# Fused layer norm, local attention and SwGLU on one core: QKV weight slices loaded in row halves, row 0's mean from two sums, and row 1's copies on ScalarE

## The chip, the cores and the metric

One core of one Trainium2 chip runs the whole program. The metric is the device time of one execution in microseconds (us). Before the change it is 503.36 us, the median of three runs (503.14 to 503.40).

## The reference

```python
xn = (x - mean(x)) / sqrt(var(x) + 1e-5)              # x: 2048 tokens x 576, bf16
q, k, v = xn @ wqkv                                   # wqkv: 576 x 1728; 32 heads of 18
logits[s, w] = q[s] . k[s - 2 w] * 18 ** -0.5         # w = 0..7, masked where s < 2 w
o[s] = sum_w softmax(logits)[s, w] * v[s - 2 w]
out = x + o @ wo + (silu(xn @ w_gate) * (xn @ w_up)) @ w_down     # hidden size 4608
```

Matmul inputs are bf16, sums are f32. The attention and the feed-forward part both start from the same normalised rows `xn`, and both results are added to `x`.

## The kernel before

The 2048 tokens are laid out as 16 "rows": partition p holds the tokens 16p to 16p+15, and row r is the tile of 128 tokens that are each partition's r-th. So a load of "x row r" is 128 partitions of 576 values (144 KB). The work has two stages. In the first, every row is normalised, transposed, and multiplied with the QKV weights. In the second, four groups of four rows (`NTT = 4`) go through gate and up matmuls (`g_pair`, line 582, matmul at line 600) in chunks of four blocks of 128 hidden units, and then through the down and output projections (`d_half`, line 615, matmul at line 629). Local attention runs on VectorE beside the matmuls (`chain`, line 400). The order of instructions on each engine is written out by hand; each engine takes its own in program order, and waits by semaphores.

The change concerns the first microseconds. What happens there, in the order of the code:

**Loads (lines 154 to 165).** DMAs are issued by two engines, each with its own queue: ScalarE ("ACT queue") and SyncE ("SP queue"). The QKV weight (576 rows by 1728 columns) is loaded in slices of 128 rows: slices 0 to 3 are one load of 432 KB each (line 149), slice 4 is the remaining 64 rows, brought in two loads, the first 864 columns to partitions 0 to 63 and the rest to partitions 64 to 127 (line 152, 108 KB each). The ACT queue gets x row 0 and then slice 1. The SP queue gets x row 1, slice 0, slice 2, x row 2, slice 3, the two pieces of slice 4, x row 3, and then three chunks of four x rows each (line 165, 576 KB each). The DMAs share eight semaphores in turn, so that an issue waits until the DMA eight places before it has landed.

**Warm-up.** TensorE multiplies constants (`warm_pe`, lines 171 to 177) until the first row is ready. ScalarE loads its table for the square root (line 166).

**Row 0 (lines 478 to 499).** Row 0 takes a short cut: it is only centred (mean subtracted) before the transpose, and the factor 1/std is applied later, when its QKV results are copied out of PSUM (`p_evac`, lines 365 and 367). VectorE takes the statistics of two halves of 288 columns and joins them (`ln_stats`: lines 214 and 218), subtracts the mean from the first 128 columns and then from the rest (`ln_center`, line 251); GpSimd centres the last 64 columns once more, as padding to 640 (line 256). TensorE transposes five blocks of 128 columns (`transp_pe`, line 262), ScalarE copies the results to SBUF in three copies (`copy_pt`, line 268) as the left operands of the QKV matmuls. Row 0 is also normalised in full (`ln_apply`, lines 240 and 243) into a buffer of its own, which a DMA transpose on the SP queue turns for the feed-forward stage (line 291).

**Row 1.** It gets its statistics, root (line 229), reciprocal (line 234) and normalising, is transposed on TensorE in three groups (column blocks 0 and 1, 2, 3 and 4), and the results are copied out by ScalarE, VectorE and ScalarE.

**QKV matmuls (line 301).** The result of a row is four PSUM tiles of 432 columns (`t` for row 0, `u` for row 1). TensorE's order is: row 0 with slice 0 (four matmuls), slice 1 (four), slice 2 for two tiles; row 1's first three transposes; row 0 with slice 2 for the other two tiles; row 1's last two transposes; row 1 with slice 0 (four); row 0 with slice 3 (four) and slice 4 (`p_row0_rest`, line 309); then the rest of row 1 (`p_row`, line 321), with row 2's transposes in its middle (`transp_halves`, line 274). PSUM has eight banks for all of this, so that row 1's tiles take the banks of the warm-up tile and of the two transpose tiles `pa` and `pb` once these are copied out.

**Rows 2 and on.** Row 2's statistics, root and normalising (lines 514 to 516) come just before the evacuation of row 0 in VectorE's order. From row 4 on the pattern is regular (lines 552 to 576).

**Later.** The V chunk of the last four rows is stored to DRAM in three pieces during the first gate and up chunk (line 672), with loads of `wd`, `wo` and the next `gu` around it.

In the profile the loads of x appear under the tile `wd` and the QKV weights under `hT`, since the buffers are shared; row 0's transposed operand is `PP`, its normalised copy `A`.

Of the kernel before, what the change touches and what calls it, by code (L numbers as in the profile page):

```python
# [10 lines left out]
f32 = mybir.dt.float32  # L11
ACT = mybir.ActivationFunctionType
ALU = mybir.AluOpType
# [4 lines left out]
P = 128  # L18
H, DH, W, DIL = 32, 18, 8, 2
D = H * DH  # L20
HALF = D // 2
# [4 lines left out]
DPAD = KT * P  # L26
# [44 lines left out]
def kernel(  # L71
# [11 lines left out]
    nc = tc.nc  # L83
# [6 lines left out]
    x_v = A_x.rearrange("b (p r) d -> p (b r) d", r=R)  # L90
    out_v = out.rearrange("b (p r) d -> p (b r) d", r=R)

    const = ctx.enter_context(tc.tile_pool(name="const", bufs=1))
# [19 lines left out]
    PP = big.tile([P, 2, RT * D], bf16, name="PP")  # L113
# [8 lines left out]
    wdf = wd[:].rearrange("p f j -> p (f j)")  # L122
    XC, XN = RT * D, RT * DPAD
    xc_b = [wdf[:, i * XC:(i + 1) * XC].rearrange("p (r d) -> p r d", d=D) for i in range(4)]
# [4 lines left out]
    wqkv = hTf[:, 0:12 * D].rearrange("p (k j) -> p k j", j=3 * D)  # L129
# [14 lines left out]
    def load_x(eng, j):  # L144
        eng.dma_start(xc_b[0][:, j:j + 1, :], x_v[:, j:j + 1, :])  # L145

    def load_w(eng, kt):
        if kt < 4:
            eng.dma_start(wqkv[:, kt, :], A_wqkv[kt * P:(kt + 1) * P, :])
        else:  # L150
            for i in range(2):
                eng.dma_start(wqkvr[64 * i:64 * i + 64, :], A_wqkv[4 * P:D, 2 * G * i:2 * G * (i + 1)])

    load_x(nc.scalar, 0)
    load_x(nc.sync, 1)
    load_w(nc.scalar, 1)
    load_w(nc.sync, 0)
    make_identity(nc, ident[:])
    load_w(nc.sync, 2)
    load_x(nc.sync, 2)  # L160
    load_w(nc.sync, 3)
    load_w(nc.sync, 4)
    load_x(nc.sync, 3)
    for c in range(1, 4):
        nc.sync.dma_start(xc_b[c], x_v[:, 4 * c:4 * c + 4, :])
    nc.scalar.activation(warm[:], eps_t[:], ACT.Sqrt)

    wp = ps.tile([P, 512], f32, name="warm_ps", tag="ps")
# [27 lines left out]
    def new_ps(name):  # L196
        return ps.tile([P, 512], f32, name=name, tag="ps")


    ln = {}  # L200

    def ln_open(c):
        mv = lns.tile([P, 4, 2], f32, name="mv")
        rstd = lns.tile([P, 4], f32, name="rstd")
        ln[c] = (xc_b[c], xn_b[c % 2], mv, rstd)

    sums = {}

    def ln_half(r, k):
        c, j = divmod(r, 4)  # L210
        xc, xn, mv, rstd = ln[c]
        if k == 0:
            sums[r] = lns.tile([P, 2, 6], f32, name="stats")
        nc.vector.bn_stats(sums[r][:, k, :], xc[:, j, k * HALF:(k + 1) * HALF])  # L214

    def ln_aggr(r):
        c, j = divmod(r, 4)
        nc.vector.bn_aggr(ln[c][2][:, j, :], sums[r][:].rearrange("p c s -> p (c s)"))

    def ln_stats(r, n=1):  # L220
        for i in range(r, r + n):
            ln_half(i, 0)
            ln_half(i, 1)
            ln_aggr(i)

    def ln_sqrt(r, n=1):
        c, j = divmod(r, 4)
        xc, xn, mv, rstd = ln[c]
        nc.scalar.activation(rstd[:, j:j + n], mv[:, j:j + n, 1], ACT.Sqrt, bias=eps_t[:], scale=1.0)

    def ln_recip(r, n=1):
        c, j = divmod(r, 4)
        rstd = ln[c][3]
        nc.vector.reciprocal(rstd[:, j:j + n], rstd[:, j:j + n])

    def ln_apply(r):
        c, j = divmod(r, 4)
        xc, xn, mv, rstd = ln[c]
        dst = xn[:, j] if r else xn0
        nc.vector.tensor_scalar(dst[:, 0:D], xc[:, j], mv[:, j, 0:1], rstd[:, j:j + 1],  # L240
                                op0=ALU.subtract, op1=ALU.mult)
        if r < 2:
            nc.gpsimd.tensor_scalar(dst[:, D:DPAD], xc[:, j, 512:D], mv[:, j, 0:1], rstd[:, j:j + 1],
                                    op0=ALU.subtract, op1=ALU.mult)
        else:
            nc.vector.tensor_copy(dst[:, D:DPAD], dst[:, 512:D])

    def ln_center(r, lo=0, hi=D):
        c, j = divmod(r, 4)
        xc, xn, mv, rstd = ln[c]  # L250
        nc.vector.tensor_scalar(xn[:, j, lo:hi], xc[:, j, lo:hi], mv[:, j, 0:1], None, op0=ALU.subtract)

    def ln_center_pad(r):
        c, j = divmod(r, 4)
        xc, xn, mv, rstd = ln[c]
        nc.gpsimd.tensor_scalar(xn[:, j, D:DPAD], xc[:, j, 512:D], mv[:, j, 0:1], None, op0=ALU.subtract)

    def transp_pe(r, kts, pt):
        c, j = divmod(r, 4)
        xn = ln[c][1]  # L260
        for i, kt in enumerate(kts):
            nc.tensor.transpose(pt[:, i * P:(i + 1) * P], xn[:, j, kt * P:(kt + 1) * P], ident[:])  # L262

    def xT_of(r):
        return xcT if r == 0 else xnT[:, :, r * P:(r + 1) * P]

    def copy_pt(eng, r, kts, pt):
        eng(xT_of(r)[:, kts[0]:kts[-1] + 1, :],
            pt[:, 0:len(kts) * P].rearrange("p (k t) -> p k t", t=P))

    def new_pt():
        return ps.tile([P, 8 * P], bf16, name="pt", tag="ps")
# [31 lines left out]
    def p_whole(r, t, kt, gs=range(NG)):  # L304
        for g in gs:
            p_mm(t, g, kt, None, r, kt == 0, False)

    def p_row0_rest(t):
        for i in range(2):
            for half in range(2):  # L310
                p_mm(t, i + 2 * half, 4, half, 0, False, True)
# [68 lines left out]
    def store(m, c, parts=1):  # L380
        st = stage[(2 * c + m - 1) % 4].rearrange("p r d -> p (r d)")
        n = XC // parts
        for i in range(0, XC, n):
            nc.sync.dma_start(kv_d[m - 1, c - 1, :, i:i + n], st[:, i:i + n])
# [82 lines left out]
    def normalize(r, n=1):  # L467
        ln_recip(r, n)
        for i in range(r, r + n):
            ln_apply(i)  # L470
            if i > 4:
                transp_dma(i)
# [3 lines left out]

    warm_pe(10, 1)
    ln_open(0)
    ln_stats(0)
    ln_center_pad(0)  # L480
    ln_center(0, 0, P)
    ln_sqrt(0)
    pa, pb = new_pt(), new_pt()
    transp_pe(0, (0,), pa)
    ln_center(0, P, D)
# [3 lines left out]
    ln_stats(1)  # L489
    ln_sqrt(1)  # L490
    copy_pt(nc.scalar.copy, 0, (3, 4), pb[:, 2 * P:])
    ln_recip(0)
    ln_apply(0)
    ln_recip(1)
    ln_apply(1)

    t = [new_ps("qkv_ps") for g in range(NG)]
    p_whole(0, t, 0)
# [2 lines left out]
    transp_pe(1, (0, 1), pt1)  # L501
    transp_pe(1, (2,), pa)
    copy_pt(nc.scalar.copy, 1, (0, 1), pt1)
    copy_pt(nc.vector.tensor_copy, 1, (2,), pa)
    p_whole(0, t, 2, (2, 3))
    transp_pe(1, (3, 4), pb)
    copy_pt(nc.scalar.copy, 1, (3, 4), pb)
    u = [None] * NG
    for g in (0, 2, 1, 3):
        u[g] = new_ps("qkv_ps")  # L510
        p_whole(1, u, 0, (g,))
    p_whole(0, t, 3)
    p_row0_rest(t)
    ln_stats(2)
    ln_sqrt(2)
    normalize(2)
    p_evac(0, t, (5, 0, 3, 2, 4, 1), dve=(5, 2))
    ln_half(3, 0)
# [88 lines left out]
    def g_evac(ch, j):  # L607
        t = ring_ps[j]
        sg = tmp.tile([P, TT], bf16, name="sg", tag="sg", bufs=3)
        uc = tmp.tile([P, TT], bf16, name="uc", tag="uc", bufs=3)  # L610
        nc.scalar.activation(sg[:], t[0][:], ACT.Silu)  # L611
        nc.scalar.copy(uc[:], t[1][:])  # L612
        nc.vector.tensor_tensor(hT[:, ch * FC + j, :], sg[:], uc[:], op=ALU.mult)  # L613
# [32 lines left out]
    for tt in range(NTT):  # L646
        for ch in range(NCH):
            it = tt * NCH + ch
            for p in range(2):
                g_pair(tt, ch, p)  # L650
                for j in (2 * p, 2 * p + 1):
                    g_evac(ch, j)
                    if it % NCH < NCH - 1 or p == 0:
                        dve.pump(1.4)
            if ch == NCH - 1:
                dve.drain(lambda: chains[0] > tt)
                for r in range(RT * tt, RT * tt + RT):
                    nc.sync.dma_start_transpose(oT[:, :, r * P:(r + 1) * P], QOP[:, r, :])
                for i in (0, 2):
                    nc.sync.dma_start(xr[:, i:i + 2, :], x_v[:, RT * tt + i:RT * tt + i + 2, :])  # L660
            if it + NSLOT < NTT * NCH:
                load_gu(it + NSLOT)
            if tt == 0:
                if 1 <= ch <= 7:
                    load_wd(ch - 1)
                if ch in (3, 4):
                    load_wd(11 - ch)
                for _ in range(3 if ch in (1, 2) else 2):
                    if wo_order:
                        load_wo(wo_order.pop(0))  # L670
                if ch == 0:
                    store(2, 3, 3)
            if ch == 1 and tt < NTT - 1:
                chain(tt + 1)
        for sub in range(0, RT, 2):
            t, fence = {}, {}
            for swap in range(2):
                for i in (sub, sub + 1):
                    d_half(tt, i, swap, t, fence)
                    if swap:  # L680
                        dve.pump(12.5 if i == sub else 4.0)
                        d_out(RT * tt + i, i, t[i])
# [30 lines left out]
```

## Time and profile before

| what | value |
|---|---|
| median of three runs | 503.36 us (503.14 to 503.40) |
| the profiled execution | 503.32 us |
| its span (first to last instruction) | 501.5 us |
| TensorE matmuls (PE) busy | 496.8 us, 99% |
| VectorE (DVE) busy | 329.0 us, 66% |
| ScalarE (ACT) busy | 200.6 us, 40% |
| granted TensorE clock | 1.0 |
| first QKV matmul | 6.01 us after the span's start |
| matmuls of line 301 (QKV) / 600 (gate, up) / 629 (down, out) | 50.1 / 280.4 / 146.4 + 22.9 us busy |

The page comes from one profiled execution. Its times are counted from the start of the span, which is 1.8 us shorter than the execution's time. A row of a time line reads: start, duration (of several merged instructions, their busy time together), engine, source line, operation, output tile, input tiles, shape, count, and in brackets how long the engine had been idle and what ended that. "SPq" and "ACTq" are instructions that issue DMAs; their duration is that of the issue, not of the transfer. In the table of stretches each line gives a stretch, the busy time of each engine with the number of instructions, and then the granted clock, the busy share of the 16 DMA engines and the GB/s that they moved. In the list of DMA issues the last number is the time from issue to landing.

### The profile page before, as it was taken

What the parts mean: (1) busy time and instruction counts of PE and PEld (TensorE: products, weight loads), DVE (VectorE), ACT (ScalarE), POOL (GpSimd) and SP (SyncE); (2) the same over time, 40 slices, a digit from 0 to 9 for tenths busy, and PEclk for the clock granted to TensorE, in tenths of its full rate; (3) what the DMA queues carried; (4) which work ended last, traced back from release to release, by engine and by line L of the source; (5) the groups of instructions that cost most, each with busy time, mean ns of one, the idle gap of its engine ahead of it and who ended that gap; (6) DMA issues with size and microseconds to landing.
All of it is one profiled execution on the core that took longest, in us unless ns stands there. A gap on an engine that the chain in (4) does not pass through costs nothing.

```text
span 501.5 us, 13267 instructions
## 1 busy us (share of the span) xinstructions
PE 496.8 (99%) x5795; PEld 282.8 (56%) x5795; DVE 329.0 (66%) x478; ACT 200.6 (40%) x415; POOL 2.6 (1%) x9
## 2 busy tenths in 40 slices
PE   8999999999999999999999999999999999999997
PEld 4555544444677644444777544445777444446775
DVE  5889597998999698999897139995980222221001
ACT  4756657645300255544300445557000454553000
POOL 2000000000000000000000000000000000000000
PEclk9999999999999999999999999999999999999999
DMA  8689989898731045535631154453700335442200
GB/s 322 164 207 228 320 268 294 260 318 272 186 114 61 25 147 185 190 112 174 166 106 47 30 182 154 131 189 110 181 26 14 106 110 177 159 126 39 76 14 25
DMA packets 77186, 75.42 MB, mean 150 GB/s; under 512 B 22708, under 2 KB 72528, under 8 KB 77128
## 3 DMA queue, kind: packets, MB, share of 16 engines
q1 hardware_dynamic: 76840, 73.98, 49.2%
q8 instruction: 45, 0.74, 0.7%
q10 hardware_dynamic: 288, 0.59, 0.3%
q14 instruction: 13, 0.11, 0.1%
HBM read 58.76 MB, written 5.90 MB: 129 GB/s over the span
## 4 chain that ended last, share of the span: by engine, by line
PE 98%; DMA 1%; DVE 0%; SPq 0%; issue 0%
PE g_ps L600 56%; PE d_ps L629 32%; PE qkv_ps L301 11%; DMA hT<-in_A_wqkv_dram 1%; DVE ot L643 0%; PE pt L283 0%; SPq L145 0%; PE pt L262 0%; PE warm_ps L262 0%
## 5 line engine op out<-in xcount | busy, mean ns | idle before, releaser
L600 PE MATMUL g_ps<-xnT,gu 64*128 64x512 bf16 x2592 | 280.4, 376 | 0.0
L600 PEld LDWEIGHTS <-gu 64*128 64x128 bf16 x2592 | 126.1, 94 | 152.9
L611 ACT ACTIVATE sg<-g_ps 128x512 bf16<-128x512 f32 x144 | 87.3, 606 | 156.6 <-PE g_ps L600 156.6
L629 PE MATMUL d_ps<-wd,hT 64*128 64x288 bf16 x2304 | 146.4, 283 | 0.0
L629 PEld LDWEIGHTS <-hT 64*128 64x128 bf16 x2304 | 112.2, 94 | 29.7
L613 DVE TENSOR_TENSOR hT<-sg,uc 128x512 bf16<-128x512 bf16 x144 | 60.0, 419 | 93.9 <-ACT uc L612 93.8
L612 ACT CAST uc<-g_ps 128x512 bf16<-128x512 f32 x144 | 85.2, 592 | 0.0
L414 DVE TENSOR_REDUCE PP<-PP 128x64 f32<-128x1152 bf16 x64 | 84.9, 1346 | 0.4
L301 PE MATMUL qkv_ps<-hT,xnT 64*128 64x432 bf16 (+1 forms) x536 | 50.1, 343 | 0.0
L409 DVE TENSOR_TENSOR PP<-QO,Kr 128x2304 bf16<-128x2304 bf16 (+1 forms) x35 | 43.5, 1249 | 7.0 <-DMA Kr<-hT 6.8
L641 DVE TENSOR_TENSOR ot<-d_ps,xr 128x288 bf16<-128x288 f32 x30 | 12.3, 450 | 51.1 <-PE d_ps L629 51.1
L441 DVE TENSOR_TENSOR PP<-Vr,A 128x2304 bf16<-128x2304 bf16 (+1 forms) x35 | 43.2, 1250 | 0.4
L301 PEld LDWEIGHTS <-xnT 64*128 64x128 bf16 (+1 forms) x536 | 25.9, 94 | 22.5 <-ACT xnT L287 0.2
L446 DVE TENSOR_TENSOR PP<-PP 128x2304 bf16<-128x2304 bf16 x24 | 32.5, 1353 | 0.3
L611 ACT ACT_TABLE_LOAD x5 | 6.4, 1283 | 47.2 <-PE g_ps L600 47.2
L629 PE MATMUL d_ps<-wo,xnT 64*128 64x288 bf16 x288 | 22.9, 283 | 0.0
L363 ACT CAST hT<-qkv_ps 128x288 bf16<-128x288 f32 (+2 forms) x58 | 21.1, 427 | 0.5 <-ACT hT L363 0.5
L434 ACT ACTIVATE PP<-PP 128x1024 f32<-128x1024 f32 x4 | 4.2, 1056 | 31.2 <-DVE PP L430 31.2
L629 PEld LDWEIGHTS <-xnT 64*128 64x128 bf16 x288 | 14.0, 94 | 3.6
L643 ACT CAST ot<-d_ps 128x288 bf16<-128x288 f32 x1 | 0.4, 399 | 38.8 <-PE d_ps L629 38.8
L363 ACT CAST QO<-qkv_ps 128x432 bf16<-128x432 f32 (+1 forms) x30 | 12.3, 409 | 7.4 <-PE qkv_ps L301 7.4
L214 DVE BATCH_NORM_STATS2 stats<-wd 128x6 f32<-128x288 bf16 x32 | 12.9, 444 | 2.8 <-DMA wd<-in_A_x_dram 2.6
(53 smaller groups left out, 89.4 us busy)
## 6 DMA issues: line engine op xcount, KB each, us to landing
gu<-in_B_w_gate_dram SPq DMA_DIRECT2D x36, 512.0 KB, 3.9
gu<-in_B_w_up_dram SPq DMA_DIRECT2D x36, 512.0 KB, 5.2
wd<-in_B_w_down_dram SPq DMA_DIRECT2D x9, 576.0 KB, 6.4
kv_d<-hT SPq DMA_DIRECT2D x5, 576.0 KB, 6.0
gu<-in_B_w_gate_dram SPq DMA_DIRECT2D x36, 64.0 KB, 5.0
gu<-in_B_w_up_dram SPq DMA_DIRECT2D x36, 64.0 KB, 4.6
xr<-in_A_x_dram SPq DMA_DIRECT2D x8, 288.0 KB, 3.9
out_dram<-ot SPq DMA_DIRECT2D x16, 144.0 KB, 1.8
```

The lines of the kernel that those rows point to most:

```text
L214: nc.vector.bn_stats(sums[r][:, k, :], xc[:, j, k * HALF:(k + 1) * HALF])
L301: return nc.tensor.matmul(t[g][:, 0:G], xT_of(r)[rows, kt, :], w_at(g, kt, rows), start=start, stop=stop)
L363: (nc.vector.tensor_copy if n in dve else nc.scalar.copy)(*parts[n])
L409: nc.vector.tensor_tensor(prod[:, a:b], QO[:, RT * tt + a:RT * tt + b, :], Kr[:, s:s + b - a, :], op=ALU.mult)
L414: nc.vector.tensor_reduce(L[:, w, rs], prod[:, rs].rearrange("p r (h d) -> p r h d", d=DH), axis=AX.X, op=ALU.add)
L441: nc.vector.tensor_tensor(dst[:, a:b], Vr[:, s:s + b - a, :].rearrange("p r (d h) -> p r d h", h=H), A[:, w, a:b].unsqueeze(2).to_broadcas ...
L446: nc.vector.tensor_tensor(dst, acc, pv, op=ALU.add)
L600: mm = nc.tensor.matmul(ring_ps[j][b][:], gu[rows, slot, k, fc], xnT[rows, kt, tok], start=(swap == 0 and kt == 0), stop=(swap == 1 and kt ...
L611: nc.scalar.activation(sg[:], t[0][:], ACT.Silu)
L612: nc.scalar.copy(uc[:], t[1][:])
L613: nc.vector.tensor_tensor(hT[:, ch * FC + j, :], sg[:], uc[:], op=ALU.mult)
L629: mm = nc.tensor.matmul(t[sub][h][:, 0:HALF], a[rows], w[rows, h * HALF:(h + 1) * HALF], start=(swap == 0 and n == 0), stop=(swap == 1 and ...
```

## The change

The changed lines do this:

- Slices 0 and 1 are loaded in row halves: rows 64 to 127 on the ACT queue, rows 0 to 63 on the SP queue, first slice 0, then slice 1. That is two more loads, one more issue on each of the two engines.
- The second and third chunk of x (rows 8 to 15) come in one load of eight rows in place of two of four.
- Row 0's mean is no longer taken from its statistics. ScalarE copies the first 288 columns with a scale of 1/576 and sums them; VectorE does the same with the other 288. The two sums `part` together are the mean, and the centring subtracts one and then the other. Both operations write their scaled copies to a scratch part of `PP`.
- Row 0's statistics are still needed for 1/std. They move behind row 1's statistics, one half ahead of row 1's normalising and one behind it; the root is taken after row 1's copies, and the reciprocal and the full normalising after row 2's statistics.
- All three copies of row 1's transposes are made by ScalarE, the second one after the last transposes.
- Row 2's statistics and root are written earlier in the code, before row 1's first matmuls; on VectorE they stand ahead of row 0's reciprocal.
- The last V store goes in two pieces in place of three.

```diff
-    load_w(nc.scalar, 1)
-    load_w(nc.sync, 0)
+    for kt in range(2):
+        for eng, lo in ((nc.scalar, 64), (nc.sync, 0)):
+            eng.dma_start(wqkv[lo:lo + 64, kt, :], A_wqkv[kt * P + lo:kt * P + lo + 64, :])
...
-    for c in range(1, 4):
-        nc.sync.dma_start(xc_b[c], x_v[:, 4 * c:4 * c + 4, :])
+    nc.sync.dma_start(xc_b[1], x_v[:, 4:8, :])
+    nc.sync.dma_start(wdf[:, 2 * XC:4 * XC].rearrange("p (r d) -> p r d", d=D), x_v[:, 8:16, :])
...
+    part = const.tile([P, 2], f32, name="part")
+
+    def ln_mean0():
+        xc = ln[0][0]
+        nc.scalar.activation(PP[:, 1, 0:HALF], xc[:, 0, 0:HALF], ACT.Copy, scale=1.0 / D, accum_out=part[:, 0:1])
+        nc.vector.tensor_scalar(PP[:, 1, HALF:D], xc[:, 0, HALF:D], 1.0 / D, None,
+                                op0=ALU.mult, op1=ALU.add, accum_out=part[:, 1:2])
...
-        nc.vector.tensor_scalar(xn[:, j, lo:hi], xc[:, j, lo:hi], mv[:, j, 0:1], None, op0=ALU.subtract)
+        nc.vector.tensor_scalar(xn[:, j, lo:hi], xc[:, j, lo:hi], part[:, 0:1], part[:, 1:2],
+                                op0=ALU.subtract, op1=ALU.subtract)
...
-    ln_stats(0)
+    ln_mean0()
     ln_center_pad(0)
     ln_center(0, 0, P)
-    ln_sqrt(0)
...
     ln_stats(1)
     ln_sqrt(1)
     copy_pt(nc.scalar.copy, 0, (3, 4), pb[:, 2 * P:])
-    ln_recip(0)
-    ln_apply(0)
+    ln_half(0, 0)
     ln_recip(1)
     ln_apply(1)
+    ln_half(0, 1)
+    ln_aggr(0)
...
     copy_pt(nc.scalar.copy, 1, (0, 1), pt1)
-    copy_pt(nc.vector.tensor_copy, 1, (2,), pa)
     p_whole(0, t, 2, (2, 3))
     transp_pe(1, (3, 4), pb)
+    copy_pt(nc.scalar.copy, 1, (2,), pa)
     copy_pt(nc.scalar.copy, 1, (3, 4), pb)
+    ln_sqrt(0)
+    ln_stats(2)
+    ln_sqrt(2)
+    ln_recip(0)
+    ln_apply(0)
...
     p_row0_rest(t)
-    ln_stats(2)
-    ln_sqrt(2)
     normalize(2)
...
-                    store(2, 3, 3)
+                    store(2, 3, 2)
```

GpSimd's centring of the padding (`ln_center_pad`) changes in the same way as `ln_center`.

More of the change, by code (lines that the diff above doesn't have):

```diff
@@ L255, in ln_center_pad @@
         xc, xn, mv, rstd = ln[c]
-        nc.gpsimd.tensor_scalar(xn[:, j, D:DPAD], xc[:, j, 512:D], mv[:, j, 0:1], None, op0=ALU.subtract)
+        nc.gpsimd.tensor_scalar(xn[:, j, D:DPAD], xc[:, j, 512:D], part[:, 0:1], part[:, 1:2],
+                                op0=ALU.subtract, op1=ALU.subtract)
     def transp_pe(r, kts, pt):
```

## The prediction

> **What bounds the kernel now.** I read the page first (busy times and slices, then the chain that ended last), then the chain restricted to the first 40 us, the time line of the first 12 us by engine, the DMA issues with their landings, and the table of stretches. The page:
>
> ```profile
> span 501.5 us, 13267 instructions
> PE 496.8 (99%) x5795; PEld 282.8 (56%) x5795; DVE 329.0 (66%) x478; ACT 200.6 (40%) x415; POOL 2.6 (1%) x9
> PE   8999999999999999999999999999999999999997
> PE 98%; DMA 1%; DVE 0%; SPq 0%; issue 0%
> ```
>
> The reader is to see that TensorE is busy in every slice but the first and last, and that the chain is TensorE and one DMA. By the table of stretches PE is busy 50.99 of the 51 us from 6 to 57, and all of the time from 57 to 498. So a change of the first microseconds is worth what it moves the continuous run of matmuls, one for one, and nothing after it gives anything back. The chain of the first 40 us says where that run begins:
>
> ```profile
> 1.17 4.79 DMA hT<-in_A_wqkv_dram
> 5.97 0.04 issue
> 6.01 1.99 PE qkv_ps L301 x10
> ```
>
> The DMA is QKV slice 0, issued at 1.17 on SP and landed at 5.96. The first QKV matmul waits for it: its left operand was there earlier (the weight load PEld L301 runs at 5.77). The next matmuls come every 0.18 us: slice 0 from 6.01, slice 1 from 6.74, slice 2 from 7.47, slice 3 (after row 1's transposes) from 9.31. What each slice leaves to spare is read from the issues (last column: us from issue to landing):
>
> ```profile
> hT<-in_A_wqkv_dram SPq DMA_DIRECT2D x1, 432.0 KB, 5.5
> hT<-in_A_wqkv_dram SPq DMA_DIRECT2D x1, 432.0 KB, 6.2
> wd<-in_A_x_dram SPq DMA_DIRECT2D x1, 576.0 KB, 7.1
> ```
>
> Slice 2, issued at 1.65, lands at 7.15, only 0.32 before its first matmul. Slice 3, issued at 2.62, lands at 8.8, 0.5 before its own. The third line is the last x chunk, issued at 7.16 and landed at 14.3. Slice 4's pieces (issued at 3.11 and 3.77, 6.3 and 5.8 to landing) are there at 9.4 and 9.6, used at 10.14.
>
> **The change part by part.** Let k0, k1, k2 be the matmuls on slices 0, 1, 2 (four, four and the first two).
>
> Loads. Before, slice 1 went on the ACT queue and slice 0 on SP, beside each other, 144 KB of x ahead of each; both landed near 6. After, both queues carry half of slice 0, then half of slice 1. If the engines keep their pace, slice 0 is whole after half of the time in which both now land (3.9, where x row 1 lands, to 5.96): near 5.0. Slice 1 is whole at 5.96 as before, and slice 2, behind the same bytes, at 7.15 as before. So k0 could come by 0.9 us earlier, k1 by 0.7, but k2 only by 0.32 less the 0.04 from landing to matmul: 0.28. **Slice 2 caps the gain**, whatever comes earlier.
>
> Whether the pace is kept is the question, since the new pieces have 64 rows. One such pair is in the trace: slice 4, two loads of 64 rows, one for each half of the partitions. The table of stretches around it:
>
> ```profile
> 4.00:6.00 2.00, 1.15 (x9) 0.52 (x7) 1.93 (x7) 0.63 (x3) 0.58 (x1) 1.00 1.03 415
> 6.00:8.00 2.00, 1.99 (x14) 1.14 (x13) 1.33 (x6) 0.86 (x3) 1.36 (x2) 1.00 1.03 391
> 8.00:9.60 1.60, 1.60 (x13) 0.90 (x11) 1.16 (x4) 0.92 (x3) 0.00 (x0) 1.00 1.10 314
> 9.60:12.00 2.40, 2.40 (x26) 1.11 (x25) 2.02 (x7) 1.59 (x5) 0.00 (x0) 1.00 1.02 413
> ```
>
> The last two columns are the DMA engines' busy share and GB/s. While the half-row pieces pass (8.0 to 9.6) the engines are as busy as ever (1.10) and move a quarter less, 314 against 414: packets wait, and not for an issue. That is 100 GB/s over 1.6 us, 160 kB, or 0.39 us for 221 kB of half rows. By landings: from 7.15 to 14.3 the queue moved 2728 kB (x row 2, slices 3 and 4, x row 3, three x chunks), 6.59 us at 414, and took 7.1: 0.5 lost. So 221 kB of half rows cost 0.39 to 0.5 us, nearly their own time at full pace (0.53). The change sends 885 kB in half rows, four times as much. From below: nothing, if the two queues, each on another half, do not meet. From above: 4 x 0.39 to 4 x 0.5, 1.6 to 2.0. I take it that an engine with both queues full serves them in turn (slices 0 and 1, one on each, were both there by 6.74), so two engines meet on the same half about half of the time, 0.8 to 1.0; and a slice is whole only with its slowest engine, which lies above the mean. I take 1.2.
>
> With it slice 0 is whole near 5.6 (half of 1.2 later than 5.0), k0 from 5.6; slice 1 at 7.2, k1 from 7.2; slice 2 at 8.35, k2 at 8.39 against 7.47: **+0.92**. Slice 3 comes at 10.0, needed at 9.31 + 0.92 = 10.23; slice 4 at 10.8, needed at 11.06. Both stay covered, so 0.92 it is. The clock through these gaps: a gap of 0.66 ahead of the first transpose left 1.00 granted, and the new ones (about 0.9 and 0.5) are of its kind.
>
> [...]
>
> Mean of row 0. Ahead of the first centring now lie two half statistics and their aggregate, 3.78 to 4.88:
>
> ```profile
> 3.78 0.82 DVE L214 BATCH_NORM_STATS2 stats<-wd 128x6 f32<-128x288 bf16 x2 [2.60 <-DMA wd<-in_A_x_dram]
> 4.63 0.21 DVE L218 BATCH_NORM_AGGREGATE mv<-stats 128x2 f32<-128x12 f32 x1
> 4.88 0.25 DVE L251 TENSOR_SCALAR wd<-wd,mv 128x128 bf16<-128x128 bf16 x1
> ```
>
> After, ACT and DVE sum 288 columns each, side by side. No row shows an operation with a sum. From below the DVE 128-column scaling, 0.25, and the ACT copy of 256, 0.37; from above ACT's 128x288 at 0.50 with a read-out like its 128x1 at 0.29, 0.79. I take 0.50, the nearest row in shape: centring at 4.3 (4.2 to 4.6) instead of 4.88, and k0's left operand, 0.89 later (4.88 to 5.77), at 5.2. ACT is free for it: a third issue of 0.46 moves its table load from 1.63 to 2.1, done with the warm-up at 3.6, before x lands at 3.75. But k0 waits for slice 0 and k2 for slice 2, so this is worth nothing on the sum; without the cover of the late slices at most the cap of 0.28 hangs on it, and of that little: from the old 5.77, k2 would be due at 7.23.
>
> Row 1's copies. DVE loses one copy of 0.22; ACT gains one of 0.27 between two of 0.37. The third copy waits for transposes which start 0.53 after the first ones (8.36 against 7.83) and begins 0.84 after them now; the added one begins about 0.6 after them and ends by then. Nothing; without that cover up to 0.27, paid by row 1's fourth matmul, whose bank the third copy empties.
>
> Row 0's statistics, root, reciprocal and normalising move behind row 1's; DVE's total is nearly the same. What waits: row 0's evacuations (first at 10.53) and, behind them in DVE's order, row 2's normalising, which ends at 10.60 now, for transposes at 11.97. The new root stands behind row 1's last copy, so row 2 is ready near 10.3 plus the delay of the slices, and those transposes move by the same delay: a cover of over 1 us. Row 0's DMA transpose is issued on SP at 11.35, behind four gu loads, and needs the normalised row by then; with the late slices the root comes near 9.9, the row near 10.6 and GpSimd's last 64 columns (0.74 from the reciprocal) near 10.9, 0.4 ahead. Behind it stand two small issues of zeros, first read by attention.
>
> SP and ACT queues. Slice 2's issue is one issue (0.45 to 0.55) later, at 2.2; it needs the queue at 6. Slice 3's issue now waits for x row 0's landing (3.75), as the second piece of slice 4 does now; it needs the queue at 7.5. Chunks 2 and 3 of x become one load; the first reader is at 25 us. The last V store goes in two pieces for three at 70.76. All nothing.
>
> **Sum.** The profiled execution took 503.32 (span 501.5 and 1.8 around it), 0.04 below the median of 503.36. 503.32 + 0.92 = 504.24, so **504.2**, of its own range 503.9 to 504.9 (slice 2 later by 0.9 to 1.9).
>
> **The rivals.**
> Full pace (the other side: faster). Mechanism: the two queues carry opposite halves, so that packets which meet now on one queue pass. For it: 415 GB/s from 4.0 to 6.0 with two queues beside each other. Then k2 comes at 7.19, capped by slice 2: 503.32 less 0.25 (0.28, less 0.03 for two more loads) is 503.07. It decides wherever slice 2 lands before 7.43.
> Full conflict: what slice 4 cost, four times at 0.5: slice 2 is 2.0 late, 505.0. For it: a single queue shows it. Against: there a queue follows one half with the other; here an engine always has the other half in its second queue.
> No effect: half the conflict I take, or less, hidden by the 0.32 that slice 2 has to spare; or full pace with sums so slow that centring starts after 4.85. 503.3.
>
> **How the numbers follow.** Forecast 0.45, full pace 0.33, full conflict 0.12, no effect 0.10. The range 502.9 to 504.9 leaves out most of full conflict and the edges. What a measurement can tell from no change is 0.2%, 1.0 us: below 502.35 or above 504.37. Full pace is capped at 0.28, so faster gets 0.02; a third of the forecast (0.14) and full conflict make slower 0.26; same 0.72.
>
> **What would show it.** In the profile after: DMA below 400 GB/s at a full busy share from 4 to 7, slice 2's landing near 8.35, PE idle before the fifth and the ninth QKV matmul. Centring by 4.3. If the DMA stays at 415 and the ninth matmul comes at 7.2, the conflict was the wrong step. PE idle after 9 us would mean a wait that I have missed.

## The result, and the profile after

The changed kernel takes 504.93 us (median of seven runs, 504.62 to 506.83), the kernel before 503.36 us (seven runs, 503.14 to 503.50). The ratio is 1.0042, 95% interval 1.0027 to 1.0057: slower by 0.4%. The forecast was 504.2. In one experiment below (the short warm-up) one execution ran at a mean granted clock of 0.658; the ratio given there leaves it out.

The profiled execution of the changed kernel took 504.62, span 502.8. The page:

```profile
span 502.8 us, 13273 instructions
PE 498.0 (99%) x5795; PEld 285.2 (57%) x5795; DVE 329.5 (66%) x479; ACT 201.0 (40%) x418; POOL 2.8 (1%) x9
PE   8999999999999999999999999999999999999997
PE 98%; DMA 1%; SPq 0%; DVE 0%; issue 0%
```

TensorE is still busy in every slice but the first and last, so the start decides again. Matmul for matmul, the ninth QKV matmul and every one behind it come 1.31 us later than before, to the last one. The span grew by the same 1.3. Nothing is lost or given back after 9 us. The chain of the first 40 us says what the start waits for:

```profile
1.80 6.08 DMA hT<-in_A_wqkv_dram
7.88 0.14 issue
8.02 1.28 PE qkv_ps L311 x6
```

The DMA is now the SP half of QKV slice 1, issued at 1.80 and landed at 7.88; before, it was slice 0, landed at 5.96. TensorE's own time line (start, busy time, what ended the idle time) shows two gaps:

```profile
6.77 0.89 PE L311 MATMUL qkv_ps<-hT,PP 128*128 128x432 bf16 x4 [0.48 <-ACT PP L278]
8.02 1.28 PE L311 MATMUL qkv_ps<-hT,PP 128*128 128x432 bf16 x6 [0.36 <-DMA hT<-in_A_wqkv_dram]
```

The second is slice 1: it starts 0.14 after that landing. The first is put down to a copy by ScalarE (6.32 to 6.69), but that copy is of column blocks that these matmuls don't read; the SP half of slice 0 landed at 6.64, 0.13 ahead of them, about the same distance. The ninth matmul follows at 8.78, just behind slice 2. Slice 1 alone would have made nearly the same delay: from 8.02, four matmuls of 0.18 bring the ninth to 8.74. Slice 2's issue (last column: us to landing):

```profile
hT<-in_A_wqkv_dram SPq DMA_DIRECT2D x1, 432.0 KB, 6.1
```

Issued at 2.67, it lands at 8.73; before, it landed at 7.15, with 0.28 to spare. **1.58 later, less 0.28, is the 1.30 that was lost.** The table of stretches shows why (last three columns: granted clock, busy share of the DMA engines, GB/s):

```profile
4.00:6.00 2.00, 1.91 (x9) 0.73 (x7) 1.46 (x6) 0.80 (x3) 0.66 (x1) 1.00 0.98 271
6.00:8.00 2.00, 1.18 (x7) 0.35 (x6) 1.86 (x7) 0.86 (x3) 0.74 (x1) 1.00 1.00 288
8.00:9.60 1.60, 1.58 (x11) 0.96 (x12) 0.64 (x3) 0.15 (x1) 0.00 (x0) 1.00 1.04 386
9.60:12.00 2.40, 2.40 (x18) 1.11 (x17) 1.86 (x8) 1.30 (x6) 0.73 (x1) 1.00 1.08 362
```

The engines are nearly as busy as before (0.98 and 1.00 against 1.03) and move 271 and 288 GB/s where they moved 415 and 391. A packet is one row of 3456 bytes in both kernels. It took 135 to 144 ns on average at this place before; while the row halves pass (3.4 to 7 us), it takes 186 to 287. From 8 us on, with the halves through, the pace is back.

The mean of row 0 did what it was meant to. In the time lines of ScalarE and VectorE:

```profile
4.41 0.44 ACT L213 ACTIVATE PP<-wd 128x288 bf16<-128x288 bf16 x1 [0.52 <-DMA wd<-in_A_x_dram]
4.76 0.19 ACT L213 ACTIVATION_READ_ACCUMULATOR PP<-wd 128x1 f32 x1
...
4.41 0.45 DVE L214 TENSOR_SCALAR_CACHE_REDUCE PP<-wd 128x288 bf16<-128x288 bf16 x1 [3.21 <-DMA wd<-in_A_x_dram]
4.79 0.09 DVE L214 DVE_READ_ACCUMULATOR PP<-wd 128x1 f32 x1
5.00 0.62 DVE L259 TENSOR_SCALAR wd<-wd,part 128x128 bf16<-128x128 bf16 x2
```

Centring starts 0.59 after row 0 is seen, against 1.10 before. But row 0 itself lands at 4.39 instead of 3.75, so the shortcut starts from a later point, and centring comes at 5.00, no earlier than the old 4.88. Row 0 is late in all five traces whose two queues begin on opposite halves (4.18 to 4.45); in the other nine it lands between 3.65 and 4.09. The cause is not shown.

### The profile page after: what moved, and what is told of

It reads as the page before. It is cut to its first block, busy times and chain, and to the rows that moved or that the text cites. A ratio compares the mean times of both kernels' runs of the same rounds, so it can differ in the third digit from the quotient of the medians.

```text
span 502.8 us, 13273 instructions
## 1 busy us (share of the span) xinstructions
PE 498.0 (99%) x5795; PEld 285.2 (57%) x5795; DVE 329.5 (66%) x479; ACT 201.0 (40%) x418; POOL 2.8 (1%) x9
## 4 chain that ended last, share of the span: by engine, by line
PE 98%; DMA 1%; SPq 0%; DVE 0%; issue 0%
PE g_ps L613 56%; PE d_ps L642 32%; PE qkv_ps L311 10%; DMA hT<-in_A_wqkv_dram 1%; SPq L158 0%; DVE ot L656 0%; PE pt L293 0%; SPq L145 0%; PE pt L272 0%; PE warm_ps L272 0%
```

## The experiments

The theory: the whole loss is the row halves. With loads of 64 partitions the DMA moved fewer GB/s here than with loads of 128 (271 against 415 from 4 to 6 us), and slice 2 queues behind them. Rivals: the price is that of the extra loads and queues, whatever their shape; or it comes from the edits of compute order. Every ratio is to the kernel before, run on the same chip.

**Whole slices, all else as changed** (also the chunk loads and the store as before):

```diff
-    for kt in range(2):
-        for eng, lo in ((nc.scalar, 64), (nc.sync, 0)):
-            eng.dma_start(wqkv[lo:lo + 64, kt, :], ...)
+    load_w(nc.scalar, 1)
+    load_w(nc.sync, 0)
```

> The changed kernel with the loads of slices 0 and 1 whole again, slice 1 on the ACT queue and slice 0 on SP, and the x chunks and the V store as before; the mean, the moved statistics and the copies stay changed. Meeting halves (theory): all of the loss is the row-half loads, so it goes; slice 2 lands near 7.15 again, the ninth QKV matmul is at 7.4 to 7.5, 503.2 to 503.5. Rival, the moved statistics and copies cost something: above 503.8, with a TensorE gap after 9 us.

Measured: 503.98 (11 runs, 503.63 to 504.50), ratio 1.0014 (1.0005 to 1.0023). The matmuls run 0.23 *earlier* than before from first to last, yet the time is longer. The last matmul starts at 497.87 instead of 498.10, and the span ends 3.94 after that start instead of 3.43 (this stretch is called the tail below). The start is cured by whole loads; something costs 0.5 at the very end. The runs on the store and on ScalarE below find it.

**The row halves alone**, in the kernel before (with the merged chunk load and the store in two):

> The kernel before with the row-half loads (and the merged x chunks and the V store in two) alone. Meeting halves: slice 2 lands at 8.7 as in the changed kernel, DMA near 280 GB/s at a full busy share from 4 to 8, 504.5 to 505.5. Rival, the loss needs the moved statistics or the mean: within 0.4 of 503.36.

Measured: 505.53 (5 runs, 504.43 to 506.32), ratio 1.0047 (1.0033 to 1.0060). In its profile slice 2 lands at 8.34 and all matmuls come 1.01 later. The stretches:

```profile
4.00:6.00 2.00, 1.39 (x7) 0.47 (x6) 1.73 (x6) 0.41 (x2) 0.58 (x1) 1.00 0.99 275
6.00:8.00 2.00, 1.47 (x10) 0.67 (x11) 1.76 (x7) 1.08 (x4) 1.03 (x2) 1.00 1.04 336
```

So the halves, without the changes of compute order, make the whole loss. (The profiled execution is the fastest of the five; the others are taken up below.)

**The same two queues and pieces, cut by columns** (128 rows, 864 columns each):

```diff
-        for eng, lo in ((nc.scalar, 64), (nc.sync, 0)):
-            eng.dma_start(wqkv[lo:lo + 64, kt, :], ...)
+        for eng, lo in ((nc.scalar, 864), (nc.sync, 0)):
+            eng.dma_start(wqkv[:, kt, lo:lo + 864], ...)
```

> The changed kernel with halves of slices 0 and 1 by columns: as many loads, as many bytes, the same two queues, but each load has 128 rows of 864 columns. Meeting halves: the DMA keeps about 400 GB/s, slice 2 lands by 7.4, 503.0 to 503.5. Rival, more and smaller loads are what costs: as slow as the changed kernel, 504.5 to 505.

Measured: 503.63 (11 runs, 503.27 to 503.99), ratio 1.0006 (0.9997 to 1.0015). Its table of stretches:

```profile
4.00:6.00 2.00, 2.00 (x11) 1.02 (x10) 1.84 (x8) 0.74 (x4) 0.66 (x1) 1.00 1.07 379
6.00:8.00 2.00, 2.00 (x14) 1.13 (x13) 1.76 (x6) 0.70 (x3) 0.74 (x1) 1.00 1.03 394
8.00:9.60 1.60, 1.51 (x11) 0.70 (x8) 1.16 (x5) 1.28 (x5) 0.17 (x1) 1.00 1.12 306
```

With as many loads and bytes on the same queues, but all 128 partitions in each, the pace is 379 and 394. Slice 0 is whole at 5.0, the ninth matmul comes 0.10 earlier. The rival of the extra loads falls. (The later matmuls come 0.41 later all the same: slice 3 and the second piece of slice 4 now land at 9.42 and 10.52, and the matmuls that wait for them start at 9.46 and 10.56. Why these loads come later is not shown: from 8 to 9.6 the pace is 306, against 314 before.)

**Both queues on the same half at once** (first rows 0 to 63 of slices 1 and 0, then rows 64 to 127):

```diff
-    for kt in range(2):
-        for eng, lo in ((nc.scalar, 64), (nc.sync, 0)):
+    for lo in (0, 64):
+        for eng, kt in ((nc.scalar, 1), (nc.sync, 0)):
```

> The changed kernel with the same four row-half loads in another order: both queues send rows 0 to 63 first (slice 0 on SP, slice 1 on ACT) and rows 64 to 127 after that, so that at any time both queues write the same half. Meeting halves: the worst case, DMA near 200 to 230 GB/s from 4 to 8, slice 2 lands at 9.0 or later, 0.3 or more later than in the changed kernel. Rival, loads of 64 rows are slow by themselves, whatever half they write: slice 2 at 8.7 as in the changed kernel.

Measured: 507.51 (4 runs, 505.58 to 507.94), ratio 1.0075 (1.0058 to 1.0093). The stretches:

```profile
4.00:6.00 2.00, 1.84 (x9) 0.88 (x7) 1.84 (x8) 0.81 (x4) 0.66 (x1) 1.00 1.01 235
6.00:8.00 2.00, 0.00 (x0) 0.00 (x0) 1.55 (x6) 0.70 (x3) 0.74 (x1) 1.00 1.01 254
8.00:9.60 1.60, 1.47 (x7) 0.77 (x8) 0.28 (x1) 0.00 (x0) 0.00 (x0) 0.85 1.04 381
9.60:12.00 2.40, 2.40 (x11) 1.28 (x10) 0.75 (x3) 0.54 (x2) 0.00 (x0) 0.50 1.07 337
```

The expected worst case (slice 2 at 9.0 or later) did not come: slice 2 lands at 8.89, against 8.73 in the changed kernel. But the two queues did not stay together. By the count of packets ScalarE begins its second half at 4.19 and SyncE at 4.95, so between these times they are on opposite halves. From 5 to 6 both send rows 64 to 127. That stretch alone, in the changed kernel and in this one:

```profile
5.00:6.00 1.00, 0.91 (x7) 0.43 (x5) 1.00 (x4) 0.27 (x1) 0.66 (x1) 1.00 1.04 297
5.00:6.00 1.00, 0.84 (x7) 0.57 (x5) 0.96 (x5) 0.39 (x2) 0.18 (x1) 1.00 1.03 235
```

So meeting on a half costs something, 297 to 235, but two thirds of the way from 415 down to 235 are there without it: the larger part of the price is that of row halves as such. The second thing to see is in the clock column: TensorE had been idle for 2.29 us, and at 9.11 its clock fell to half for 3.41 us, which doubled the time of the matmuls there:

```profile
8.13 2.83 PE L311 MATMUL qkv_ps<-hT,PP 128*128 128x432 bf16 x10 [2.29 <-DMA hT<-in_A_wqkv_dram]
```

**Halves of every second row** (64 partitions again, spread over all 128):

```diff
-        for eng, lo in ((nc.scalar, 64), (nc.sync, 0)):
-            eng.dma_start(wqkv[lo:lo + 64, kt, :], ...)
+        for eng, lo in ((nc.scalar, 1), (nc.sync, 0)):
+            eng.dma_start(wqkv[lo:P:2, kt, :], ...)
```

> The changed kernel with halves of 64 rows again, but every second row (even rows on SP, odd rows on ACT), so that each load spans all the partitions. Meeting halves: faster loads than in the changed kernel, DMA above 330 GB/s from 4 to 8, slice 2 by 7.9. Rival, loads of 64 rows are slow by themselves: slice 2 at 8.7, DMA near 280.

Measured: 504.51 (9 runs, 503.89 to 505.05), ratio 1.0023 (1.0014 to 1.0033). The DMA moves 296 and 375 GB/s from 4 to 8, slice 2 lands at 8.13 and the ninth matmul comes 0.70 later. So which 64 partitions are taken does matter: spreading them gives back a good third of slice 2's delay (0.98 left of 1.58), but not all.

**Row halves for slice 0 only** (slice 1 whole on SP behind it; one more ScalarE instruction at the start, for a reason that comes below):

```diff
-    for kt in range(2):
-        for eng, lo in ((nc.scalar, 64), (nc.sync, 0)):
-            eng.dma_start(wqkv[lo:lo + 64, kt, :], ...)
+    for eng, lo in ((nc.scalar, 64), (nc.sync, 0)):
+        eng.dma_start(wqkv[lo:lo + 64, 0, :], ...)
+    load_w(nc.sync, 1)
```

> The changed kernel with row halves for QKV slice 0 alone; slice 1 goes whole on SP behind the half of slice 0, and ScalarE does its warm-up root twice, so that its code fetch keeps away from the last store. Theory (the loss goes by the bytes that are sent in half rows): half as many, so slice 2 lands 0.6 to 0.9 later than before (7.75 to 8.05 for 7.15), the ninth QKV matmul comes 0.3 to 0.65 later than before, and the median is 503.6 to 504.2. Rival (the first meeting of the two halves, while x is still loading, costs nearly all of it): slice 2 lands at 8.3 or later, median 504.4 or more.

Measured: 504.62 (5 runs, 504.19 to 505.90), ratio 1.0032 (1.0017 to 1.0046). Slice 2 lands at 8.86, 1.71 later than before, with half as many bytes in row halves. The theory of a price per byte falls; the numbers are those that were expected of the rival, that the first meeting of the halves costs nearly all. The stretches say what happens:

```profile
3.40:4.20 0.80, 0.80 (x4) 0.24 (x3) 0.00 (x0) 0.08 (x1) 0.00 (x0) 1.00 1.01 190
4.20:5.20 1.00, 1.00 (x4) 0.23 (x2) 0.72 (x4) 0.54 (x2) 0.20 (x1) 1.00 1.15 214
5.20:6.00 0.80, 0.77 (x6) 0.45 (x5) 0.80 (x4) 0.27 (x1) 0.46 (x1) 1.00 0.67 168
6.00:7.00 1.00, 0.28 (x4) 0.08 (x2) 0.93 (x4) 0.73 (x3) 0.00 (x0) 1.00 1.01 370
```

The last packet of ScalarE's half is begun at 4.14, and it has landed at 5.24; from then on the SP queue is alone, at 214 GB/s and then 168, together 194 from 4.2 to 6: **half the pace of a whole load (415)**. (The busy share counts a packet where it begins: 1.15 and 0.67 are long packets that run over 5.2, and over both stretches it is 0.93.) By the count of packets, the 64 rows of the SP half are all begun at 4.84, and the first rows of slice 1, whole, are in the slow part too; why they are slow is left open. Only from 6 on does slice 1 pass at 370. In the same stretch, 4.2 to 5.2, the two opposite halves of the changed kernel moved 259. So row halves took 259 to 297 as two opposite halves, 235 on one side and 214 alone. (The first 0.8 us of two opposite halves are slower still, 190 here and 186 in the changed kernel, against 251 where both queues begin on one half; that is left open, too.) Two opposite halves at once are 20 to 40% above one alone (259 to 297, against 214).

This kernel's profiled execution, 505.85, shows a second cost:

```profile
6.95 3.48 PE L312 MATMUL qkv_ps<-hT,PP 128*128 128x432 bf16 x10 [0.72 <-ACT rstd L238]
...
11.01 0.90 PE L312 MATMUL qkv_ps<-hT,xnT 128*128 128x432 bf16 x4
```

Ten matmuls in 3.48 us are 0.36 apart, four in 0.90 are 0.18 apart: until 10.01, where its record of the granted clock begins, TensorE ran at half speed (the column of the table shows 1.00 only because the record has nothing before that). The ninth matmul came at 9.79, 0.93 after slice 2.

**The gaps of the changed kernel filled**: two matmuls on constants ahead of the first QKV matmul, two ahead of the fifth.

```diff
     t = [new_ps("qkv_ps") for g in range(NG)]
+    warm_more(2)
     p_whole(0, t, 0)
+    warm_more(2)
     p_whole(0, t, 1)
```

> The changed kernel with two more constant matmuls (into the warm-up tile) ahead of row 0's matmuls on slice 0 and two ahead of those on slice 1, so that TensorE works through the gaps. If the spread of the changed kernel (504.6 to 506.8) comes from a TensorE clock that is lowered after gaps in some executions: all runs within 0.5 of 504.7, clock 1.0 in each. If it comes from the loads: the spread stays at about 2 us. The four matmuls stand in gaps of 0.7 and 0.5, so they may cost up to 0.3.

Measured: 504.65 (8 runs, 504.54 to 505.25; one run is 0.05 beyond what was expected), ratio 1.0029 (1.0019 to 1.0039), every run's mean clock 1.00. The seven runs of the changed kernel lie over 2.2 us, these over 0.7. The two slowest of the changed kernel (506.43 and 506.83) are the two with a mean clock of 0.997: 0.003 x 503 us, twice over for half speed, is 3.0 us, about one stretch of 3.41. The mean does not tell of a clock that opens late: the execution of 505.85 above has a mean of 1.00, since its record begins at 10.01.

**The row halves alone, gaps filled** (the second run above, with the same four matmuls):

> The kernel before with the row halves (and what goes with them: one load for x chunks 2 and 3, the last store in two), and two matmuls on constants ahead of the first QKV matmul and two ahead of the fifth, in TensorE's idle time. Theory (part of the spread with row halves is TensorE's clock, which idle time ahead of those matmuls can close for one stretch): every run has the granted clock at 1.00, the runs lie within 0.7 us of each other, and the median is 504.2 to 504.8, against 505.53 without the four matmuls. Rival (the spread comes from the loads, whose meeting differs from run to run): the spread stays near 2 us and the median stays at 505 or above.

Measured: 504.67 (10 runs, 504.41 to 505.35), ratio 1.0027 (1.0017 to 1.0036), mean clocks 0.999 to 1.00. The spread falls from 1.9 to 0.9, a little over the 0.7 expected, and the median by 0.86. What is left, 1.3, is the late slice 2 (here 8.92, all matmuls 1.57 later in the profiled execution). So the halves cost twice: 1.3 by the loads, and in some executions up to 2 more, which the filled gaps take away. That this is a half-speed stretch is shown for the runs with a mean clock of 0.997; for the others (505.04 to 505.69 at 1.00 without the four matmuls) it is not shown.

**Half the warm-up, in the kernel before** (5 matmuls on constants instead of 10):

> The kernel before with five of the ten long warm-up matmuls, so that TensorE is idle from about 3 to 5 us. If an idle stretch there keeps TensorE at half speed longer: QKV matmuls 0.36 apart instead of 0.18 for 1 us or more, 504 to 506, and a spread of more than 0.8. Rival, TensorE's speed does not depend on what it did before: 503.3.

Measured: 505.10 (504.99 to 505.26, four runs), ratio 1.0035 (1.0022 to 1.0049), 1.76 more than the kernel before on that chip. The time is as expected, the spread (0.27) is not. The fifth execution, the only one with a trace, took 753.71. Its QKV matmuls are 0.36 apart from 6.23 until the clock opens at 8.76; that the four others lost their 1.76 by such a late opening is inferred. From 8.76 to the end its granted clock is 0.65:

```profile
core 0: 751.9 us, clock 0.658
```

It is one execution; why the clock stayed there isn't known.

**The loss at the end: whole slices, with the chunk load and the store as changed**:

> The changed kernel with slices 0 and 1 whole, and with the merged x chunks and the V store in two pieces left as changed (12 loads ahead of gu, so other code and other turns of the semaphores than in e1_whole). If the 0.7 of e1_whole came from its end (an instruction fetch beside the last store): 503.0 to 503.4. If the moved statistics and copies cost it: 503.8 to 504.2 again.

Measured: 504.23 (11 runs, 504.01 to 505.40), ratio 1.0020 (1.0011 to 1.0029). The number is the one that was expected if the moved statistics and copies cost it, but the trace says otherwise: all matmuls stand where they stood before, to 0.01 us, and the whole difference is the tail, 4.29 us instead of 3.43. The transfers from 498 to 502 us (the queue, and the last store with its us to landing):

```profile
q14 instruction: 1, 0.01, 1.1%
...
out_dram<-ot SPq DMA_DIRECT2D x1, 144.0 KB, 2.5
```

A fetch of instructions (8 KB on queue 14) is begun at 499.90, beside the last store, which lands 2.5 after its issue instead of 1.7. Before, that fetch came at 502.56, after the end; in the changed kernel at 478.53, far ahead of it. In the fourteen traces its place goes with the number of ScalarE's instructions (an issue of a DMA counts): with 574 or 575 of them it comes after the end, with 578 (here and in the first experiment) beside the last store, with 579 (the changed kernel) between 477 and 481.

**One more ScalarE instruction** (the square root of the warm-up done twice), in this kernel and in that of the first experiment:

```diff
     nc.scalar.activation(warm[:], eps_t[:], ACT.Sqrt)
+    nc.scalar.activation(warm[:], eps_t[:], ACT.Sqrt)
```

> e8_whole2 with one more ScalarE instruction at the start (the warm-up root a second time), which moves ScalarE's later instructions one place on in its code. If e8_whole2's loss is the instruction fetch beside the last store: the fetch (8 KB, at 499.9 there) comes near 478 as in the changed kernel, the end after the last matmul takes 3.4 again instead of 4.3, 503.2 to 503.5. If the moved statistics and copies cost it: 504.2 again.

> e1_whole with the same one instruction. If its loss is the fetch: 502.9 to 503.4, so with the mean and the copies changed, and whole loads, no slower than the kernel before. If the moved statistics and copies cost it: 504.0 again.

Measured: 503.46 (11 runs, 503.24 to 504.06), ratio 1.0003 (0.9994 to 1.0012), and 503.38 (11 runs, 503.13 to 503.59), ratio 0.9999 (0.9990 to 1.0008). The fetch has moved to 477 in both, the tails are 3.48 and 3.43, and the last store of the first takes its old time:

```profile
out_dram<-ot SPq DMA_DIRECT2D x1, 144.0 KB, 1.7
```

So the mean from two sums, the moved statistics, the copies on ScalarE, the merged load and the store together cost nothing and bring nothing. No version tried beats the kernel before by more than the measurement can tell.

## Why the prediction was right in kind and wrong in size

- **What bounds it: right.** The delay at the ninth matmul is the delay at the end, 1.31, one for one.
- **Slice 2 as the place: right.** Slice 2's landing less 0.28 of slack gives the loss in the profile of the changed kernel. With the halves alone (slice 2 1.19 later, 1.01 lost) 0.1 of it is slice 1's: its first matmul came at 7.75, and the ninth followed four matmuls behind it, at 8.47. The forecast had slice 1 whole at 7.2; it came at 7.88 and 7.61.
- **The step that failed: the size of slice 2's delay.** The forecast took 1.2 (slices 0, 1 and 2 whole at 5.6, 7.2 and 8.35); the changed kernel showed 1.58 (6.64, 7.88 and 8.73), and the other kernels with the same halves 1.19 and twice 1.77. Most of it is lost early. From 3.4 to 8 us, in stretches that end at 4.2, 5.2, 6, 7 and 8, the pace was 415, 415, 415, 393 and 389 GB/s before and 186, 259, 302, 256 and 320 in the changed kernel. Worked out from these, 1.0 us is lost before 6 us and 0.5 behind it. The 1.2 came from "two engines meet on the same half about half of the time". The runs put another thing in its place: a row half is slow by itself, whoever else is on (214 GB/s alone, from 4.2 to 5.2 us with slice 0 in halves). Two opposite halves, which the forecast counted as free, gain a quarter over two on one side (297 to 235 GB/s from 5 to 6 us) and are still far below 415. The bounds worked out from slice 4's pair, 1.6 to 2.0, hold three of the four delays to within 0.02; the discount for opposite queues is what failed. The 1.9 at the upper end of the forecast's own range is shown by no run: the runs showed 1.58, 1.19 and twice 1.77, and 1.71 with slice 0 alone in halves.
- **The second step that failed: the clock.** "The new gaps are of its kind" carried one gap of 0.66 that had left the clock alone over to two of 0.48 and 0.36. In the profiled execution that held; in two of the seven runs the mean clock (0.997) shows one stretch lost, and the filled gaps took the outliers away. By the medians (504.93 against 504.65) this is 0.3 of the loss, less than the intervals of the two ratios can tell apart; in single runs it is up to 2. What closes the clock in those runs stays open: none of them has a trace, and the last section shows it closing only behind longer idle times (2.00 us and more). Without the lost clock the time lay inside the range, as the profiled execution's 504.62 does; with it the range, which ended at 504.9, was short at its upper end.
- **The mean of row 0 worth nothing: right**, but for a further reason: row 0 landed 0.64 later, which the prediction had not counted. The sums took 0.54 to the end of ScalarE's read-out, against 0.50 taken; centring came at 5.00, not 4.3. With whole slices and the merged load, row 0 is early, and centring came at 4.25; but slice 0 at 5.97 held the first matmul, and no matmul moved.
- **Covers: right.** Slice 3 (10.37, used at 10.62) and slice 4 (11.18, used at 11.45) stayed hidden. Row 1's three copies on ScalarE (9.45 to 10.36) held up none of its matmuls. Row 2 was normalised at 11.96; its transposes load their weights from 13.28 on.
- **The rivals.** Full pace: refuted by 271 GB/s. No effect: refuted. Full conflict, 505.0 with slice 2 late by 2.0: the result lies by its number, but by a delay of 1.58 with some lost clock, not by 2.0.

Left open: why the same row halves delay slice 2 by 1.2 in one execution and 1.8 in another; why row halves on spread partitions are still below full pace; why two opposite halves begin so slowly; whether the half-speed stretches of the single runs come from the gaps in each case, since only two were caught in a trace.

## What to carry to other kernels

Cut a load by columns, not by partitions, when it is to go over two queues: the same bytes came at 379 GB/s in 128-row pieces and at 271 in 64-row pieces. Here even that brought nothing over whole slices (503.63 against 503.29 before). Before a load that is early enough is made earlier, look at the one behind it in the queue and at its slack (here 0.28), and at what else shares the DMA engines then (row 0, 0.64 late). When a difference of half a microsecond can't be found at the start, compare the tails.

## What the runs showed of the hardware that was not expected

- **TensorE's granted clock went by stretches of 3.41 us** (in the fourteen traces every record of the granted clock but the last lasts a whole number of them). In these traces the granted clock first opened between 3.6 and 6.2 us from the start in twelve, at 8.76 with the half warm-up, and at 10.01 in the run with slice 0 in halves; in one it closed for exactly one stretch (9.11 to 12.53) after the idle 2.29 us. At half speed, such a stretch is worth 1.7 us of matmuls (an estimate, half of 3.41). In the traces it closed at the end of stretches in which TensorE was idle for 2.29 us (above), and for 2.00, 2.05 and 2.87 us at the ends of the runs with column halves, whole slices and every second row. It stayed open behind 1.79 us (whole slices and the merged load, at the end) and less.
- **A fetch of 8 KB of instructions beside the last store costs 0.5 to 0.9 us** (the tails of 3.94 and 4.29 against 3.43), and a single instruction on ScalarE decides whether it falls there (504.23 against 503.46). That it is ScalarE's code is inferred from the counts and from what the one instruction did.
- **The granted clock can stay at 0.65 for a whole execution on one core** (753.71 us for 505.10), seen once.
- **Accumulating operations end here with a read-out of their own**: 0.19 on ScalarE, 0.09 on VectorE, behind 0.44 and 0.45 for 128x288.
